# Loads in flight, the last store and the program's order in an RWKV-5 and SwiGLU kernel

## The chip, the cores and the metric

The kernel runs on one core of one Trainium2 chip. The metric is the device time of one execution in microseconds (us); lower is better. The core has a matrix engine (TensorE, PE in the profile; its weight loads are listed as PEld), VectorE (DVE), ScalarE (ACT), GpSimd (POOL) and SyncE (SP), which here issues nearly all transfers. Every engine works through its own queue of instructions in order. An instruction that must wait for another engine or for a transfer holds back everything behind it in its queue.

## The reference

An attention block without softmax (RWKV-5) is followed by a feed-forward block. There are 4 batches, 8 heads, 768 tokens and 48 channels a head, and all data are fp32 on the device.

```
for t in range(S):                                  # S = 768
    cur = einsum('bhd,bhe->bhde', u * k[t], v[t])
    y[t] = einsum('bhd,bhde->bhe', r[t], state + cur)
    state = w * state + einsum('bhd,bhe->bhde', k[t], v[t])

x = y as (3072 tokens, 384 features)
xn = x / sqrt(mean(x * x) + 1e-6) * rms_g
g, val = xn @ w_gate, xn @ w_val                    # 384 -> 1536
out = (g * sigmoid(g) * val) @ w_out                # 1536 -> 384
```

The weights w_gate, w_val and w_out reach the device as 64-bit floats, eight bytes each.

## The kernel before

The sequence is cut into 12 chunks of 64 tokens. With four batches a chunk holds 256 tokens. For each chunk `mixing(s)` does the attention. TensorE computes, with the names that the planner gives the steps:

- E: products of r with u*k, which give the diagonal of the scores (chunks 0 and 1 only; later chunks use VectorE steps called bonus1 to bonus3, which read the table `utab`)
- A: the scores inside the chunk. VectorE then writes the diagonal (d) and the masked scores (m) into the tile MT
- Y: the outputs, from V and MT and, after chunk 0, from the state ST carried over
- U: the update of the state, from V and KH, where KH is the tile TOK scaled by VectorE (step h)
- r, spread: sums of squares for the normalisation, and their distribution over the partitions

V, the tile for r and k by channel (`chan`, CH) and the tile for k by token (TOK) exist once each. A load for the next chunk can start only when the last reader of the chunk before has finished.

The feed-forward block then takes the 256 tokens of a chunk. Chunks 0 and 1 use plain products: the steps g (gate and value, `gate_val`, two TensorE steps each of 1.29 us) and P (`project`). The weights come in 26 pieces while these two chunks are computed. A piece (`piece`, line 395) is loaded by SP into one of six raw buffers. ACT computes a rounding part from the lower word (ulp), VectorE two steps from the upper word (bits1, bits2), and GpSimd adds the two (sum), so that an fp32 weight results. Pieces 0 to 17 are gate and value weights, pieces 18 to 25 the output weights (wot).

From chunk 2 on, two chunks are taken together. The first layer uses seven products instead of eight for each pair (steps f1 to f7 in `group`, six groups a pair), and the second layer likewise (P1 to P7 in `second_layer`). In this part the weights are read once more to check their range (`check`, steps "look"). The products use three banks of the accumulator memory, a, b and c, and a fourth tile, `at`, serves the attention.

The order of the program is written out by hand. Each step is registered with a planner (`Plan.add`, line 191): its engine, an estimated cost, the names it reads and writes, and a function that gives the instructions. The list `ORDER` (lines 83 to 155) then states in which order the 1532 steps are given to the engines. Since each engine works in order, the list decides what stands ahead of what in each queue, and at most how early a step can start. The planner's costs are used only to choose the number of warm-up products at the start. The waits between engines follow from which tiles are read and written.

A further wait is put on loads by hand. `InOrder.at_most` (line 164) lets a load go only when the load n places before it in the same sequence has landed:

```
made = give()
self.flying.append(made.ins)
if len(self.flying) > n:
    self.tc.add_manual_dep(made.ins, self.flying.pop(0).name, ...)
```

Loads of `chan`, TOK, V and the weight pieces pass through it, with n = IN_FLIGHT (line 258: `FIRST, IN_FLIGHT = 2, 2`). The load of `utab`, the moves of a few rows inside the on-chip memory (`move_heads`), the range checks and the stores do not, but they stand in the same SP queue.

At the end, `second_layer` of the last pair (chunks 10 and 11) works in two halves, js = 0 and js = 1. `result` (line 1171) stores each finished piece. For the last pair SP stores the first 64 rows and ACT the other 64; for other pairs SP stores both.

Of the kernel before, what the change touches and what calls it, by code (L numbers as in the profile page):

```python
# [72 lines left out]
def feature_order():  # L73
# [10 lines left out]
    0, 9, 1, 5, 14, 4, 2, 3, 6, 11, 12, 19, 39, 16, 8, 17, 40, 44, 41, 43, 24, 15, 49, 46, 47, 10, 42, 29, 20, 50, 74,  # L84
    45, 7, 51, 56, 13, 48, 53, 96, 57, 52, 18, 58, 54, 21, 55, 22, 63, 60, 26, 59, 27, 64, 23, 34, 25, 65, 81, 61, 66,
    62, 99, 28, 30, 67, 82, 119, 68, 109, 31, 69, 122, 70, 120, 75, 104, 36, 32, 86, 101, 76, 114, 83, 33, 84, 121,
    77, 100, 191, 35, 102, 78, 123, 80, 87, 98, 79, 71, 105, 190, 124, 37, 73, 127, 38, 187, 91, 130, 125, 103, 129,
    128, 92, 72, 126, 110, 106, 131, 107, 97, 115, 88, 108, 132, 151, 111, 133, 116, 152, 112, 117, 270, 153, 135,
    113, 380, 136, 206, 118, 137, 159, 154, 93, 134, 138, 160, 193, 196, 139, 155, 161, 192, 140, 145, 141, 142, 156,
    188, 215, 143, 148, 157, 162, 275, 144, 163, 214, 197, 164, 189, 194, 158, 171, 165, 211, 201, 146, 198, 172, 147,  # L90
    212, 199, 167, 173, 166, 195, 285, 174, 168, 202, 150, 213, 200, 89, 175, 149, 218, 176, 203, 169, 208, 221, 272,
    216, 237, 217, 183, 170, 268, 271, 204, 177, 184, 209, 178, 205, 280, 179, 185, 94, 186, 223, 273, 243, 267, 220,
    277, 90, 207, 244, 278, 222, 210, 180, 245, 224, 246, 219, 274, 251, 181, 281, 182, 252, 348, 349, 247, 253, 276,
    350, 279, 317, 225, 254, 287, 312, 226, 351, 248, 238, 229, 302, 263, 230, 361, 95, 255, 249, 282, 307, 227, 250,
    85, 256, 288, 228, 283, 264, 257, 258, 284, 265, 231, 239, 266, 259, 304, 286, 352, 260, 360, 309, 357, 305, 298,
    261, 232, 262, 290, 310, 289, 294, 233, 240, 303, 242, 269, 308, 299, 306, 241, 358, 295, 332, 311, 300, 301, 296,
    353, 318, 322, 297, 314, 291, 354, 319, 359, 337, 355, 387, 315, 292, 388, 327, 293, 374, 391, 389, 324, 408, 313,
    356, 323, 392, 320, 390, 407, 325, 362, 234, 316, 363, 399, 393, 321, 328, 236, 366, 364, 334, 367, 400, 326, 333,
    365, 339, 564, 561, 368, 342, 369, 329, 335, 340, 330, 562, 338, 343, 563, 331, 375, 370, 376, 336, 573, 341, 344,
    565, 371, 381, 382, 345, 406, 394, 346, 377, 568, 409, 379, 439, 378, 570, 395, 347, 587, 440, 384, 396, 410, 418,  # L100
    397, 566, 372, 383, 593, 401, 235, 373, 398, 567, 411, 413, 571, 594, 569, 402, 574, 412, 572, 385, 386, 575, 405,
    577, 441, 447, 442, 403, 414, 404, 444, 448, 576, 443, 445, 588, 449, 415, 579, 450, 446, 458, 620, 580, 453, 451,
    459, 454, 581, 460, 455, 452, 457, 466, 461, 621, 463, 467, 582, 468, 456, 462, 464, 477, 465, 583, 589, 472, 469,
    473, 474, 481, 470, 476, 478, 624, 479, 471, 485, 480, 622, 482, 486, 475, 416, 417, 487, 590, 483, 419, 421, 484,
    420, 496, 623, 630, 424, 488, 578, 491, 489, 595, 497, 498, 492, 591, 493, 490, 504, 495, 633, 499, 500, 505, 506,
    422, 494, 423, 501, 592, 632, 427, 515, 502, 425, 426, 503, 507, 430, 510, 508, 516, 517, 511, 646, 512, 509, 523,
    514, 518, 524, 625, 629, 525, 584, 520, 627, 513, 519, 428, 521, 429, 534, 522, 626, 433, 631, 431, 526, 628, 432,
    529, 527, 436, 535, 653, 536, 530, 531, 528, 533, 542, 537, 652, 543, 553, 634, 532, 554, 635, 539, 556, 636, 538,
    540, 544, 545, 647, 541, 637, 638, 548, 546, 639, 547, 549, 599, 551, 550, 437, 552, 596, 640, 555, 600, 641, 597,
    602, 559, 557, 434, 558, 435, 607, 598, 601, 648, 438, 797, 586, 642, 603, 643, 608, 798, 560, 611, 606, 604, 644,  # L110
    605, 585, 655, 645, 799, 656, 806, 610, 612, 807, 800, 803, 613, 649, 609, 654, 683, 801, 651, 685, 684, 614, 650,
    810, 691, 804, 615, 823, 809, 802, 692, 658, 830, 617, 805, 808, 829, 693, 657, 686, 618, 811, 856, 616, 857, 812,
    688, 813, 687, 689, 659, 694, 690, 619, 697, 695, 815, 696, 702, 816, 698, 703, 817, 699, 662, 704, 701, 710, 705,
    858, 707, 711, 700, 818, 706, 708, 712, 713, 709, 859, 660, 716, 661, 721, 717, 665, 714, 718, 826, 720, 715, 722,
    719, 723, 663, 664, 729, 724, 668, 860, 726, 730, 824, 731, 725, 727, 862, 825, 732, 728, 735, 733, 740, 736, 737,
    739, 742, 741, 863, 748, 743, 734, 882, 666, 745, 667, 738, 749, 671, 744, 746, 750, 751, 747, 759, 752, 827, 753,
    754, 760, 757, 761, 755, 828, 756, 669, 767, 758, 762, 869, 670, 861, 768, 674, 672, 764, 888, 673, 763, 765, 770,
    766, 769, 677, 773, 771, 831, 778, 774, 775, 777, 780, 779, 868, 782, 772, 781, 675, 776, 676, 783, 864, 866, 680,
    786, 784, 889, 865, 785, 789, 787, 788, 867, 792, 814, 793, 835, 790, 794, 678, 819, 791, 820, 836, 837, 870, 795,
    796, 832, 871, 839, 833, 679, 822, 874, 681, 682, 1033, 843, 872, 875, 1036, 821, 873, 842, 840, 841, 876, 844,  # L120
    846, 877, 834, 878, 879, 847, 891, 880, 881, 1037, 1046, 1045, 883, 838, 848, 849, 884, 892, 850, 894, 851, 885,
    1034, 852, 919, 1035, 921, 920, 887, 886, 1039, 927, 845, 1043, 1059, 895, 1038, 1040, 893, 1066, 928, 853, 922,
    929, 1041, 1065, 854, 938, 890, 924, 896, 855, 923, 925, 897, 930, 926, 933, 931, 939, 898, 940, 934, 901, 935,
    932, 937, 946, 941, 1042, 936, 942, 947, 948, 1044, 943, 957, 944, 945, 949, 952, 950, 959, 953, 1092, 954, 958,
    1047, 956, 951, 960, 955, 1060, 965, 1095, 1049, 962, 1048, 961, 963, 966, 968, 964, 899, 900, 1051, 971, 967,
    902, 969, 1061, 976, 1052, 972, 903, 973, 907, 1053, 977, 975, 978, 904, 970, 984, 979, 974, 981, 985, 1054, 980,
    982, 986, 987, 983, 1093, 990, 1094, 995, 988, 991, 989, 1062, 996, 1096, 992, 997, 908, 994, 1105, 1003, 905,
    998, 906, 1118, 1000, 1102, 910, 993, 1067, 1004, 999, 1001, 1101, 1005, 1006, 1002, 1125, 1099, 1064, 1098, 1014,
    1007, 1063, 909, 1009, 1015, 913, 1104, 1016, 1010, 1050, 1011, 1008, 1013, 1097, 1017, 911, 1124, 1103, 1022,
    1012, 1019, 1023, 912, 1018, 1020, 916, 1024, 1025, 1021, 914, 915, 1028, 1026, 1027, 1029, 1071, 1100, 1030,  # L130
    1055, 1031, 1072, 1056, 1073, 1106, 1032, 1068, 1119, 1075, 1058, 1069, 1107, 1120, 1110, 1111, 1108, 1079, 1269,
    1272, 917, 918, 1070, 1076, 1077, 1112, 1080, 1082, 1113, 1109, 1273, 1114, 1057, 1078, 1083, 1115, 1270, 1271,
    1074, 1127, 1279, 1084, 1117, 1085, 1282, 1086, 1116, 1087, 1121, 1275, 1081, 1128, 1155, 1130, 1156, 1088, 1089,
    1122, 1295, 1123, 1302, 1129, 1274, 1157, 1163, 1158, 1090, 1160, 1164, 1091, 1278, 1165, 1159, 1126, 1161, 1166,
    1162, 1134, 1174, 1167, 1280, 1131, 1169, 1175, 1168, 1176, 1170, 1171, 1173, 1182, 1177, 1178, 1183, 1281, 1184,
    1172, 1179, 1135, 1193, 1180, 1276, 1181, 1185, 1328, 1188, 1186, 1187, 1195, 1189, 1132, 1277, 1133, 1197, 1191,
    1190, 1137, 1194, 1192, 1301, 1196, 1283, 1329, 1285, 1198, 1201, 1199, 1200, 1204, 1202, 1330, 1136, 1203, 1207,
    1284, 1140, 1205, 1335, 1212, 1208, 1287, 1209, 1214, 1213, 1211, 1138, 1296, 1216, 1215, 1288, 1206, 1332, 1217,
    1139, 1210, 1289, 1218, 1220, 1141, 1219, 1331, 1223, 1221, 1142, 1222, 1226, 1146, 1224, 1143, 1231, 1227, 1286,
    1228, 1230, 1233, 1232, 1225, 1235, 1290, 1234, 1229, 1236, 1239, 1237, 1238, 1242, 1240, 1241, 1144, 1245, 1243,  # L140
# [104 lines left out]
def fast(ctx, tc, chan, tok, vpad, wka, wkb, wot, cols, u_row, out, bad):  # L245
# [9 lines left out]
    wide = wka.dtype == I64  # L255
    PIECE = NQ * CC * P

    FIRST, IN_FLIGHT = 2, 2
    NT = B * L
    const = ctx.enter_context(tc.tile_pool(name="const", bufs=1))  # L260
    work = ctx.enter_context(tc.tile_pool(name="work", bufs=2))
# [880 lines left out]
    def second_layer(s):  # L1142

        last = s + 2 == NS
# [636 lines left out]
```

## Time and profile before

| | |
|---|---|
| time, median of 3 runs | 608.51 us (605.94 to 609.43) |
| time of the profiled execution | 608.8 us |
| its span (first to last instruction) | 607.0 us |
| TensorE busy | 587.4 us |
| VectorE, ScalarE, GpSimd busy | 417.9, 297.1, 41.3 us |
| bytes moved, mean rate over the span | 62.99 MB, 104 GB/s |
| landing of a 576 KB weight piece, of V (512 KB), of chan (1024 KB), median | about 5.0, 4.3, 6.7 us |

All instructions of the kernel have line L178 in the profile, since `InOrder` gives them all from that line; they are told apart by the tiles that they write and read. A bracket after a timeline entry gives the idle time of the engine ahead of it and what released it. SPq and ACTq are the queues that issue transfers. "PEclk" is the share of full clock that TensorE was granted.

### The profile page before, as it was taken

The numbers are of one execution on the slowest core, as the hardware profiler recorded it, in microseconds if no ns is written. First come the engines' busy times: TensorE is split into PE (matmuls) and PEld (weight loads), VectorE is DVE, ScalarE is ACT, GpSimd is POOL, SyncE is SP. The second block draws the span as 40 slices with busy tenths as digits, with TensorE's granted clock in tenths as the row PEclk, the third lists the DMA queues.
The fourth block names the chain that finished last, engine by engine and source line by source line (L and its number), as shares of the span: only waits on it lengthen the run. The fifth ranks groups of instructions, "written<-read, shape, count | busy, mean of one in ns | idle before, by whom it ended". The sixth has DMA issues, their size and how long they took to land.

```text
span 607.0 us, 16431 instructions
## 1 busy us (share of the span) xinstructions
PE 587.4 (97%) x7202; PEld 516.4 (85%) x7202; DVE 417.9 (69%) x621; ACT 297.1 (49%) x721; POOL 41.3 (7%) x40
## 2 busy tenths in 40 slices
PE   5979999999999999999999999999999999999995
PEld 3768888667888899888899988899989899988895
DVE  6686886688777798566698466698567685455541
ACT  5653667635557554365465256564156762123200
POOL 3241322230000000000000000000000000000000
PEclk8689999999999999999999999999999999999999
DMA  6786754505132404411501602601422210200011
GB/s 209 243 257 218 252 172 143 179 2 208 53 94 72 163 2 119 143 54 50 218 22 36 240 1 60 235 15 34 154 96 87 65 44 23 70 27 28 1 28 31
DMA packets 22544, 62.99 MB, mean 104 GB/s; under 512 B 2976, under 2 KB 9792, under 8 KB 21056
## 3 DMA queue, kind: packets, MB, share of 16 engines
q1 hardware_dynamic: 21840, 61.46, 30.9%
q8 instruction: 58, 0.95, 0.7%
q10 hardware_dynamic: 624, 0.39, 0.2%
q14 instruction: 22, 0.18, 0.1%
HBM read 56.04 MB, written 4.72 MB: 100 GB/s over the span
## 4 chain that ended last, share of the span: by engine, by line
PE 92%; DMA 5%; ACT 1%; issue 0%; SPq 0%; DVE 0%; ACTq 0%
PE bank_b L178 32%; PE bank_a L178 26%; PE bank_c L178 24%; PE at L178 10%; DMA V<-in_vpad_dram 2%; DMA chan<-in_chan_dram 1%; DMA raw<-in_wot_dram 1%; DMA raw<-in_wkb_dram 1%; ACT ulp L178 0%; ACT ku L178 0%; ACT wk L178 0%; SPq L178 0%; ACT m L178 0%; DVE MT L178 0%; ACT h L178 0%
## 5 line engine op out<-in xcount | busy, mean ns | idle before, releaser
L178 DVE TENSOR_TENSOR gv<-bank_b,m 128x512 f32<-128x512 f32 x90 | 62.2, 691 | 66.5 <-PE bank_b L178 61.9
L178 ACT ACTIVATE gv<-gv 128x256 f32<-128x256 f32 (+1 forms) x60 | 30.7, 521 | 71.9 <-DVE gv L178 71.8
L178 DVE TENSOR_TENSOR gv<-bank_c,gv 128x512 f32<-128x512 f32 x60 | 41.5, 691 | 24.6 <-PE bank_c L178 24.1
L178 PE MATMUL bank_b<-xa,wa 64*128 64x256 f32 x444 | 56.2, 386 | 0.0
L178 PEld LDWEIGHTS bank_b<-xa,wa 64*128 64x128 f32 x444 | 43.3, 191 | 5.5 <-issue 0.2
L178 ACT COPY m<-bank_a 128x512 f32<-128x512 f32 (+1 forms) x35 | 19.9, 569 | 55.6 <-PE bank_a L178 33.5
L178 PE MATMUL bank_a<-wo,h 128*128 128x192 f32 x264 | 46.0, 330 | 0.5 <-ACT m L178 0.5
L178 PE MATMUL bank_a<-xa,wa 64*128 64x256 f32 x372 | 46.4, 379 | 0.0
L178 PE MATMUL bank_a<-xb,wb 64*128 64x256 f32 x372 | 45.7, 378 | 0.0
L178 PE MATMUL bank_b<-t,wb 64*128 64x256 f32 x360 | 44.3, 376 | 0.8 <-issue 0.8
L178 PE MATMUL bank_b<-t,s 64*128 64x256 f32 x360 | 44.8, 381 | 0.0
L178 PEld LDWEIGHTS bank_a<-wo,h 128*128 128x128 f32 x264 | 42.8, 190 | 2.3 <-issue 1.3
L178 PE MATMUL bank_c<-xb,s 64*128 64x256 f32 x360 | 44.3, 376 | 0.1
L178 PE MATMUL bank_c<-t,s 64*128 64x256 f32 x360 | 44.1, 377 | 0.0
L178 ACT ACTIVATE MT<-dmask,du 128x64 f32<-128x64 f32 x160 | 40.9, 336 | 5.3 <-DVE du L178 5.2
L178 ACT ACTIVATE rows_out<-rows_out 128x384 f32<-128x384 f32 x72 | 39.7, 557 | 2.3 <-DMA rows_out<-in_wot_dram 1.5
L178 PEld LDWEIGHTS bank_a<-xa,wa 64*128 64x128 f32 x372 | 36.1, 187 | 4.1 <-issue 0.2
L178 PEld LDWEIGHTS bank_a<-xb,wb 64*128 64x128 f32 x372 | 35.7, 187 | 4.5 <-issue 0.3
L178 PEld LDWEIGHTS bank_b<-t,wb 64*128 64x128 f32 x360 | 35.2, 187 | 4.8 <-issue 0.9
L178 DVE TENSOR_TENSOR h<-gv 128x256 f32<-128x256 f32 (+1 forms) x60 | 32.7, 552 | 9.2 <-ACT gv L178 9.2
L178 PEld LDWEIGHTS bank_c<-xb,s 64*128 64x128 f32 x360 | 35.4, 187 | 4.0 <-issue 0.3
L178 PEld LDWEIGHTS bank_b<-t,s 64*128 64x128 f32 x360 | 34.4, 187 | 5.0 <-issue 1.2
(179 smaller groups left out, 1079.1 us busy)
## 6 DMA issues: line engine op xcount, KB each, us to landing
chan<-in_chan_dram SPq DMA_DIRECT2D x11, 1024.0 KB, 6.7
TOK<-in_tok_dram SPq DMA_DIRECT2D x10, 768.0 KB, 5.2
V<-in_vpad_dram SPq DMA_DIRECT2D x12, 512.0 KB, 4.3
raw<-in_wot_dram SPq DMA_DIRECT2D x8, 576.0 KB, 5.1
rows_out<-in_wka_dram SPq DMA_DIRECT2D x12, 384.0 KB, 3.3
rows_out<-in_wkb_dram SPq DMA_DIRECT2D x12, 384.0 KB, 3.2
rows_out<-in_wot_dram SPq DMA_DIRECT2D x12, 384.0 KB, 3.1
out_dram<-rows_out SPq DMA_DIRECT2D x41, 96.0 KB, 2.2
```

Of the source, the lines that this page charges most:

```text
L178: return lambda *args, **kwargs: self.tc.keep_in_program_order(give(*args, **kwargs))
```

## The change

Three things change. The number of loads that may be in flight goes from two to four. Of the last pair, the last piece that is stored (k = 1, second half) is stored by ScalarE alone, both sets of 64 rows; all other stores stay where they were. And the list ORDER is another permutation: it has 1531 entries, since the last piece has one store step instead of two. The step names of the stores get individual keys, which only the planner reads.

```
-    FIRST, IN_FLIGHT = 2, 2
+    FIRST, IN_FLIGHT = 2, 4
...
-            if last:
-                add("SP", 0.6, keys, ["stored"], lambda: give((0,), sp), land=2.5, name="store")
-                add("ACT", 0.6, keys, ["stored'"], lambda: give((1,), act), land=2.5, name="store")
+            if last and k == 1 and js == (1,):
+                add("ACT", 1.0, keys, [f"stored {s} {k} {js}'"], lambda: give((0, 1), act), land=2.5, name="store")
+            elif last:
+                add("SP", 0.6, keys, [f"stored {s} {k} {js}"], lambda: give((0,), sp), land=2.5, name="store")
+                add("ACT", 0.6, keys, [f"stored {s} {k} {js}'"], lambda: give((1,), act), land=2.5, name="store")
             else:
-                add("SP", 1.2, keys, ["stored"], lambda: give((0, 1), sp), land=2.5, name="store")
+                add("SP", 1.2, keys, [f"stored {s} {k} {js}"], lambda: give((0, 1), sp), land=2.5, name="store")
```

What the new list does to each queue, by the names of the steps (the first ones, and the places that the prediction uses):

```
TensorE start   before  E0 A0 E0 Y0 A0 Y0 r0 r0 g g spread wk g E1 U0 g A1 g g Y1 ...
                after   E0 E0 A0 A0 Y0 Y0 r0 r0 g g spread wk g g U0 E1 A1 g g Y1 ...
TensorE, chunk 3   before  A3 g g g g g Y3 P(1,0) P(1,1) r3 P(0,0) ...
                   after   A3 P(0,0) Y3 P(1,0) P(1,1) r3 P(0,1) ...
TensorE end     before  P1 P1 flag P2 P6 P4 P7 P5 P6 P3 P7 P4 P5 P3
                after   flag P1 P1 P4 P6 P5 P7 P2 P6 P4 P7 P3 P5 P3
VectorE start   before  ... K R d m R d m bits1 2 ...
                after   ... K bits2 0 R R d m d m bits1 3 ...
VectorE, chunk 3   before  ... m3 bits2 20 hm h3 bits1 22 m3 ...
                   after   ... bits2 21 m3 m3 bits1 23 bits1 22 ...
SP loads        before  0, k0, 1, r0, 2, V0, 3, 4, TOK0, chan1, 5, 6, 8, 7, 9, 10, V1, utab, chan2, TOK1, 14, 13, move1, 11, TOK2 ...
                after   k0, 1, 0, r0, 2, V0, 3, 4, 6, chan1, 5, TOK0, 8, 7, 9, V1, TOK1, 11, 10, 12, TOK2, 14, move1, chan2, 15, 13, utab ...
```

Numbers alone are weight pieces; a number after k, r, V, TOK or chan is the chunk.

## The prediction

> **What bounds the kernel now.** I read the page first (busy times, slices, chain), then windows of 2 us for the first 64 us, then the timeline of the stretches that stood out, then the end. From the page:
>
> ```profile
> PE 587.4 (97%) x7202; PEld 516.4 (85%) x7202; DVE 417.9 (69%) x621; ACT 297.1 (49%) x721; POOL 41.3 (7%) x40
> ...
> PEclk8689999999999999999999999999999999999999
> ```
>
> TensorE is busy 587.4 of 607.0 us, so only 19.6 us are idle, and its work isn't changed. What an order or earlier loads can save is idle time and time at a lowered clock. The windows of 50 us show 48.92, 50.00, 49.25, 50.00 ... 49.93 us busy from 100 us on; nearly all the loss is in the first 46 us and at the end. The clock line says the same: 8, 6, 8 tenths in the first three slices, then 9. The 2 us windows (columns: window, length, busy us and instruction count of PE, PEld, DVE, ACT, POOL, then granted clock, DMA share, GB/s):
>
> ```profile
> 12.00:14.00 2.00, 0.67 (x27) 0.48 (x20) 1.95 (x5) 0.99 (x4) 0.74 (x1) 0.50 0.78 253
> 14.00:16.00 2.00, 1.88 (x70) 1.91 (x73) 0.00 (x0) 0.26 (x1) 0.00 (x0) 0.50 0.57 167
> ...
> 26.00:28.00 2.00, 1.54 (x10) 0.93 (x10) 0.93 (x3) 1.22 (x5) 0.93 (x1) 1.00 0.95 362
> ...
> 36.00:38.00 2.00, 1.41 (x14) 0.92 (x10) 1.97 (x5) 1.98 (x3) 0.72 (x2) 1.00 0.86 271
> 38.00:40.00 2.00, 0.00 (x0) 0.00 (x0) 2.00 (x3) 0.06 (x1) 0.78 (x1) 1.00 0.76 251
> 40.00:42.00 2.00, 1.35 (x93) 1.38 (x97) 2.00 (x3) 0.00 (x0) 1.73 (x1) 1.00 1.03 383
> 42.00:44.00 2.00, 2.00 (x55) 1.77 (x46) 1.56 (x3) 0.80 (x1) 1.42 (x2) 0.52 0.60 223
> 44.00:46.00 2.00, 2.00 (x14) 1.60 (x14) 0.00 (x0) 1.69 (x5) 0.00 (x0) 0.63 0.71 180
> ```
>
> The reader is to see two things. TensorE stands still from about 37.4 to 40.6, and afterwards runs at about half clock until 45. And the transfers mostly run at 170 to 270 GB/s, though single windows reach 362 and 383. The timeline names the waits:
>
> ```profile
> 14.12 1.56 PE L178 MATMUL at<-MT,V 64*64 64x64 f32 x48 [1.46 <-DMA V<-in_vpad_dram]
> 15.43 1.10 PE L178 MATMUL bank_a<-RR,chan 48*64 48x64 f32 x32
> ...
> 17.12 1.88 PE L178 MATMUL bank_c<-MT,V 64*64 64x64 f32 x48 [0.58 <-DVE MT L178]
> ...
> 40.65 1.16 PE L178 MATMUL at<-MT,V 64*64 64x64 f32 x64 [3.24 <-DMA V<-in_vpad_dram]
> ...
> 108.48 1.16 PE L178 MATMUL at<-MT,V 64*64 64x64 f32 x64 [1.08 <-ACT ulp L178]
> ```
>
> Both early waits are for V, the operand of the "Y" products of chunks 0 and 1. The third is Y of chunk 3, whose mask (ready at about 108.3) stood on VectorE behind a conversion that waited 3.10 us for a wot load. The SP timeline shows why V came late: V of chunk 0 was issued at 9.69, when the load before the last one had landed, and V of chunk 1 at 35.15, behind a weight load that was held the same way, although its buffer had been free since U of chunk 0 at 31.6.
>
> **What the Trainium skill says.** "DMA: Bandwidth & Descriptors", section "Anatomy of one DMA", gives a fixed part of about 2.0 us beside bytes over 436 GB/s. The trace agrees in kind: the 10 KB load of col took 1.7 us, the 576 KB loads 5.0. Two such loads in flight (1.18 MB in 4.9 us) give 241 GB/s, near the 261 GB/s measured from 20 to 40 us: the limit of two holds the rate down, not the memory. "TensorE: Matmul & The Clock Gate", part 1, says the clock falls to half after about 3.4 us idle and returns after about 3.4 us busy; here 3.2 us idle was followed by clocks of 0.52 and 0.63 for 4 us. "TensorEngine Tiling (Array Packing)", "Key Properties", says a change of tiling mode drains the engine; here the first product after an attention block takes 1.50 us instead of 1.29, so 0.2 us a change. "Runtime: NRT & Kernel Launch", "Instruction fetch mechanics", says a taken branch outside the fetched window forces a fetch; at the end here SP and ACT branch at 601.5 and go on at 605.1 and 605.3.
>
> **The change part by part.** The instruction lists of the two programs, engine by engine, hold the same work: 369 TensorE steps in both, and only the last stores are shared out differently.
>
> *Four loads in flight and the new order, first 46 us.* I walk the chain by hand. New issue order: k, wkb, wka, r of chunk 0 at once, then wka, V, wkb, wka. Up to r are 1.83 MB, up to V 2.75 MB. With the first load at 1.25, 1.7 us to the first landing and some 360 GB/s, r lands at about 8 to 9 (before 9.69), V at 10.6 to 12 (before 14.07). TensorE's order becomes E, E, A, A, Y, Y, so the second A no longer stands behind the Y that waits for V. VectorE then runs R, R, d, m, d, m without a hole: from 9.1, with the measured 1.21, 0.69, 0.74, 0.78, 0.74, 0.78, the last mask is ready at 14.0. Before, it came after A at 15.43 and Y started at 17.12. So the second Y starts at 14.0, 3.1 us earlier. It ends at 15.9 (1.88), its squares on ACT at 16.6, the second half of the row sums (half of 2.72) at 18.0; before, these ended at 21.64. The first weight product starts 3.6 us earlier and ends 3.5 earlier. Its exchanged copies (four of 0.51 after yT at 17.4) end at 19.5, before its second half needs them.
>
> From there to Y of chunk 1, TensorE had 11.3 us of work (26.1 to 37.4), so it is ready at about 33.9. V of chunk 1 can be issued once U of chunk 0 has read the old one, about 28.2, and a V load took 3.5 to 5.4 us: 31.7 to 33.6. The 3.24 us wait goes. TOK of chunk 0 is three places later on SP; 5.96 MB at 300 GB/s land at 23, and it is needed at 26. So Y starts 6.7 us earlier. Without the hole the clock stays up: Y took 2.51 in the chain and the pair after it 3.96, against 1.99 and 2.79 at full clock, 1.7 us in all. Together 8.4 us.
>
> Next late would be VectorE: it was busy 9.97 of 10 us from 30 to 40, and now has the same conversions to do some 8 us earlier, in one queue in which a conversion waiting for a load holds back masks and bank releases. Its total of 113 us in the first 150 leaves room (81% of 140), but not at every point. The bounds of this part are 0, if the time is lost again to such holds, and 8.4. I take three quarters, 6.3.
>
> *Y of chunk 3.* In the new VectorE list both masks stand ahead of the two waiting conversions, and one projection step is put before Y. The 1.08 us goes: 1.1 (bounds 0 and 1.1; next late would be the wot piece of that projection, whose loads were there by 91 before).
>
> *Mode changes.* Counted in both lists: 93 before, 89 after, at 0.2 us: 0.8. The chain of waits shows the price:
>
> ```profile
> 79.79 1.99 PE at L178 x128
> 81.78 1.50 PE bank_c L178 x12
> 83.28 1.29 PE bank_a L178 x12
> ```
>
> Elsewhere in the steady part TensorE has no hole to close, so its other moves count nothing; the banks' readers (VectorE 31 to 41 us busy per 50) hide them. If that cover were gone, each late bank costs one product, 1.3 us.
>
> *The last 35 us.* P1 is followed by P2 in the same bank, which waits for a copy on ACT:
>
> ```profile
> 576.32 0.48 ACT L178 COPY m<-bank_a 128x384 f32<-128x384 f32 x1 [2.19 <-PE bank_a L178]
> ...
> 576.85 4.17 PE L178 MATMUL bank_a<-wo,h 128*128 128x192 f32 x24 [0.51 <-ACT m L178]
> ```
>
> In the new order P4 comes between, and the flag product is moved ahead of P1. P4 reads what h23 wrote (before: by 575.2), P6 needs sum_2; the new VectorE order adds g2 before g1, so sum_2 ends at about 577.5 instead of 578.8, before P6 at 578.2. Gain 0.5 (bounds 0 and 0.6).
>
> *The last store.* Before, SP and ACT issued half each at 600.9, 0.47 and 0.50 us. Now ACT issues both, so its branch comes 0.5 us later, at 602.0; SP has branched earlier and does its waits meanwhile. Behind ACT's second issue stands only the end. Bounds: +0.5 (ACT's 3.8 us after the branch ends the program) and -0.5 (SP's eight semaphore steps of 605.1 to 605.6 were the last thing). I take +0.2. New names for the planner's store keys issue nothing.
>
> *Sum.* Against the profiled execution's own 608.8 us (span 607.0 and 1.8 around it): 608.8 - 6.3 - 1.1 - 0.8 - 0.5 + 0.2 = 600.3. The median of the runs, 608.51, is 0.3 from it; I leave 600.3. Had everything come in: 598.2.
>
> **The rivals.** *VectorE takes over.* Only the wait for V goes, 3.2 us and 0.3 of the clock; the conversions then set the pace and the head start melts. With 1.1 from mode changes and the end that is 4.6: 604.2. For it: 9.97 of 10. Against it: VectorE idles 5.47 us just after, until 49.1, waiting for TensorE.
>
> *Nothing moves.* The limit isn't what holds the loads; buffers are (six raw buffers, one V, one chan, one TOK). Then only mode changes and the end remain, 1.1: 607.7. For it: SP also waits for engines. Against it: in the first 20 us the SP timeline shows issues exactly at landings.
>
> *Slower.* The table of u (utab) is ten places later on SP, behind the load of chan for chunk 2, and VectorE's step bonus2, which reads it, now stands ahead of the release of the first bank of chunk 1's products. Up to utab are 14.2 MB. By the walk above TensorE is out of banks if that release comes after 56.2, so utab must land by 53.3 (bonus2 0.95, bonus3 0.94, state 0.54, release 0.42): 280 GB/s. Each us later is a us of TensorE, and such a hole costs 1.7 for the clock again. At 225 GB/s from 2.5 us on it lands at 65.6, 12.3 late: 598.2 + 14.0 = 612.2. The gain is eaten up below 238 GB/s, a little less than two loads in flight reached from 20 to 40 us.
>
> **How the numbers follow.** Forecast 600.3 (597 to 603): 0.60. VectorE takes over, 604.2 (603 to 606): 0.17. Nothing moves, 607.7: 0.15. Slower, 612.2: 0.08. A measurement of this kernel can tell about 0.5%, 3 us, from no change: faster is below 605.5, slower above 611.5. Faster: 0.60 + 0.14 + 0.01 = 0.75; same 0.03 + 0.14 = 0.17; slower 0.08. The range of 8 in 10 goes from 597 to 606.5: the first two cases and a little of the third.
>
> **What would show it.** Right: V of chunk 0 landed by 12, first weight product at 18, Y of chunk 1 by 34 to 36 without a wait for V, a clock of 1.00 from then on, f1 of chunk 2 (135.5 before) at 125 to 128, no ACT wait between P1 and what follows. Wrong: holes on TensorE between 40 and 110 released by VectorE, a DMA rate still near 240 GB/s, or conversions that wait for raw buffers.

## The result and the profile after

| | before | after |
|---|---|---|
| median of the runs made together | 608.94 us (605.94 to 609.43) | 599.2 us (596.28 to 599.99) |
| profiled execution | 608.8 us | 599.91 us |
| its span | 607.0 us | 598.2 us |
| mean granted clock | 0.985 | 0.993 |

The ratio of the times is 0.9842, with a 95% interval from 0.9802 to 0.9883. The forecast was 600.3 us. The profiled execution of the changed kernel was one of its longer ones, so its trace shows less than the medians do: 8.9 us of 9.7. The page of the changed kernel:

```profile
PE 583.4 (98%) x7202; PEld 512.6 (86%) x7202; DVE 411.2 (69%) x621; ACT 296.2 (50%) x721; POOL 46.2 (8%) x40
...
PEclk8989999999999999999999999999999999999999
```

TensorE is idle 14.8 us now (598.2 - 583.4), after 19.6. The second slice, which had a clock of 6 tenths, has 9, and the third has 8 as before. The 2 us windows, with the same columns as before, say where:

```profile
12.00:14.00 2.00, 1.89 (x94) 1.70 (x87) 2.00 (x7) 0.85 (x2) 1.71 (x2) 0.73 0.88 334
...
34.00:36.00 2.00, 1.10 (x77) 1.01 (x68) 1.97 (x4) 0.06 (x1) 0.00 (x0) 1.00 1.00 400
36.00:38.00 2.00, 1.17 (x41) 1.02 (x40) 1.60 (x3) 0.00 (x0) 1.32 (x1) 0.75 0.94 269
38.00:40.00 2.00, 2.00 (x13) 1.65 (x12) 0.00 (x0) 1.91 (x4) 1.62 (x2) 0.50 0.84 296
```

TensorE's timeline of the same stretch, where the two brackets with V are gone:

```profile
13.30 0.91 PE L178 MATMUL at<-MT,V 64*64 64x64 f32 x48
...
18.00 1.57 PE L178 MATMUL bank_a<-yT,wa 64*128 64x256 f32 x12
...
33.57 1.16 PE L178 MATMUL at<-MT,V 64*64 64x64 f32 x64
...
37.98 2.74 PE L178 MATMUL bank_b<-xa,wa 64*128 64x256 f32 x12
```

Y of chunk 1 starts at 33.57 instead of 40.65, at full clock. But from 36 to 40 the clock is 0.75 and 0.50, and the product that follows Y takes 2.74 us where it would take 1.57. The chain of waits (start, length, what) shows what lies between:

```profile
33.64 1.47 PE at L178 x89
35.10 1.73 issue
36.83 1.22 PE at L178 x39
38.05 3.96 PE bank_b L178 x23
```

(A shorter stop of this kind, 0.86 us, lies in the second Y of chunk 0, at 15.3.) In the middle of Y of chunk 1, after 89 of its 128 products, TensorE stands for 1.73 us. "issue" means that nothing which the profile shows is waited for. The kernel before has no such stop in this Y, and no step of the prediction has it.

The whole difference, from the start times of the same steps in both traces:

| stretch | before | after | gain |
|---|---|---|---|
| start to Y of chunk 1 | 40.65 | 33.57 | 7.1 |
| from there to the first g step of chunk 1 (g 1 0 0) | 15.56 | 17.54 | -2.0 |
| to Y of chunk 2 | 23.51 | 23.51 | 0 |
| to f1 of chunk 2 | 55.68 | 54.51 | 1.2 |
| to P1 of chunks 10 and 11 | 436.66 | 434.82 | 1.8 |
| to the last matmul | 28.13 | 27.24 | 0.9 |
| last matmul to the end of the span | 6.8 | 7.0 | -0.2 |

The sum is 8.8 us, the difference of the spans.

### The profile page after: what moved, and what is told of

The parts are those of the page before. It is cut to its first block, busy times and chain, and to the rows that moved or that the text cites. A ratio compares the mean times of both kernels' runs of the same rounds, so it can differ in the third digit from the quotient of the medians.

```text
span 598.2 us, 16446 instructions
## 1 busy us (share of the span) xinstructions
PE 583.4 (98%) x7202; PEld 512.6 (86%) x7202; DVE 411.2 (69%) x621; ACT 296.2 (50%) x721; POOL 46.2 (8%) x40
## 4 chain that ended last, share of the span: by engine, by line
PE 94%; DVE 2%; ACT 1%; issue 1%; DMA 1%; POOL 0%; SPq 0%; DVEq 0%; ACTq 0%
PE bank_b L178 32%; PE bank_a L178 26%; PE bank_c L178 26%; PE at L178 10%; DMA chan<-in_chan_dram 1%; DVE RR L178 1%; DVE bits L178 0%; ACT ku L178 0%; DVE MT L178 0%; ACT up L178 0%; DVE ms L178 0%; ACT ST L178 0%; DVE KH L178 0%; POOL ms L178 0%; SPq L178 0%
## 5 line engine op out<-in xcount | busy, mean ns | idle before, releaser
L178 ACT ACTIVATE gv<-gv 128x512 f32<-128x512 f32 (+1 forms) x60 | 31.2, 524 | 72.5 <-DVE gv L178 71.8
L178 PEld LDWEIGHTS bank_c<-t,s 64*128 64x128 f32 x360 | 34.6, 187 | 4.3 <-DVE h L178 0.3
```

The costliest lines, as they stand in the source:

```text
L178: return lambda *args, **kwargs: self.tc.keep_in_program_order(give(*args, **kwargs))
```

## The experiments

The whole set, with the intervals of the ratio to the kernel before. The column "f1" is the start of f1 of chunk 2 in the profiled execution, "steady" the time from there to P1 of the last pair, "end" from there to the last matmul.

| run | loads | order up to f1 | order after it | time | ratio, 95% | span | f1 | steady | end |
|---|---|---|---|---|---|---|---|---|---|
| before | 2 | old | old | 607.85 | | 607.0 | 135.4 | 436.7 | 28.1 |
| old_order_four | 4 | old | old | 600.76 | 0.9844 to 0.9937 | 595.0 | 124.3 | 435.5 | 28.1 |
| new_order_two | 2 | new | new | 606.9 | 0.9966 to 1.0007 | 602.4 | 134.1 | 434.8 | 27.2 |
| new_order_three | 3 | new | new | 600.94 | 0.9872 to 0.994 | 594.6 | 125.9 | 434.8 | 27.2 |
| front_new_rest_old | 4 | new | old | 600.93 | 0.9843 to 0.9926 | 599.3 | 127.5 | 436.9 | 28.1 |
| front_old_rest_new | 4 | old | new | 598.32 | 0.9819 to 0.9891 | 598.2 | 128.6 | 435.5 | 27.3 |
| new_order_old_store | 4 | new | new | 600.77 | 0.9849 to 0.9922 | 599.9 | 131.3 | 434.8 | 27.3 |
| hold_11 | 4 | new | new | 598.12 | 0.9821 to 0.9881 | 596.4 | 127.9 | 434.8 | 27.2 |

The runs were made on three chips, each beside the kernel before. Its median was 607.85 us for the first four, 606.83 for front_old_rest_new and new_order_old_store, and 606.48 for hold_11. So the times of different groups are compared by their ratios only. The spans and "f1" are those of one execution: it was the fastest of its kernel in old_order_four, new_order_two and new_order_three, and a longer one in the changed kernel.

The column "f1" differs by up to 4 us between executions of nearly the same program: f1 is at 129.1 in the changed kernel, at 131.3 with the old store alone and at 127.9 in hold_11. The clock of the first 20 us differs too: 0.91, 0.83 and 0.74 in these three. So the first columns of one profile don't tell two of these kernels apart; the intervals do, or the presence of a wait. The last two columns repeat to 0.1 us where no stop and no wait falls into them.

**The limit alone** (old_order_four).

```
-    FIRST, IN_FLIGHT = 2, 2
+    FIRST, IN_FLIGHT = 2, 4
```

> The order and the last store of before, four loads in flight. If the limit on loads is what gave the time (my theory for the front): V of chunk 0 lands by 12 us and V of chunk 1 by 36, Y of chunk 1 starts 4 to 6 us earlier than 40.65, and the whole is 4 to 6 us faster than before, 603 to 605. If the order gave it and the limit is only needed in company: the second A still stands behind Y, raw buffers hold the loads, and less than 2 us are gained, 607 to 609.

The time is 1.1% below the kernel before, 7.1 us where 4 to 6 were expected. The whole change gave 1.6%, and the two intervals overlap. The chain of waits of this run from 29 us on:

```profile
29.60 2.79 PE bank_c L178 x24
32.39 1.99 PE at L178 x128
34.38 2.79 PE bank_b L178 x24
```

Y of chunk 1 is ready at 32.3 with the old order too, there is no stop within its 128 products, and the clock stays up. The first weight product starts at 17.05, against 21.57. The wait ahead of Y of chunk 3 is gone as well: from Y of chunk 2 to f1 are 54.52 us.

**The order alone** (new_order_two): the changed kernel, its last store included, with the limit set back.

```
-    FIRST, IN_FLIGHT = 2, 4
+    FIRST, IN_FLIGHT = 2, 2
```

> Everything of the changed kernel but the limit, which is two. If the order alone gave the time: within 2 us of the changed kernel, 598 to 601. If the limit did: V of chunk 1 lands late again, TensorE waits 3 us or more ahead of Y of chunk 1, the table of u or a weight piece holds VectorE later on, and the time is 605 to 612.

The interval holds no change; the order alone is worth at most 0.34%, 2 us. The first weight product starts at 22.18, later than before (21.57). TensorE's timeline shows what came in place of the old wait for V:

```profile
36.08 1.16 PE L178 MATMUL at<-RR,chan 48*64 48x64 f32 x64 [2.12 <-DVE chan L178]
37.17 2.90 PE L178 MATMUL bank_c<-yT,wa 64*128 64x256 f32 x12
...
41.65 1.16 PE L178 MATMUL at<-MT,V 64*64 64x64 f32 x64
```

A of chunk 1 waits for VectorE's work on chan, the clock falls, and the product behind it takes 2.90 us. Y of chunk 1 starts a microsecond later than in the kernel before. From Y of chunk 2 to f1 are 54.51 us, so the order alone removes the wait ahead of Y of chunk 3, just as the limit alone does.

**Three loads** (new_order_three): the same line with `IN_FLIGHT = 3`.

> The changed kernel with three loads in flight. In the changed kernel TensorE stood 1.73 us inside Y of chunk 1 with no wait that the profile shows, at the first instruction of a block of 256 of its own queue (number 1217). If loads in flight slow the fetch of instructions, this hole shrinks with three, below 1 us, and the clock stays up; the time is the same or up to 2 us better, 597 to 599. If the depth of the queue of loads has nothing to do with the hole, it stays at 1.5 us or more wherever Y of chunk 1 still starts before 34.5 us, and the time is 599 to 602.

Three give what four give, within what the timing tells. The stop in Y is gone, as the theory had it, but the 597 to 599 us expected with it did not come. A of chunk 1 waits 2.39 us here, so the front isn't a clean comparison with four.

**The two halves of the order** (front_new_rest_old, front_old_rest_new). Both have four loads in flight. The first takes the new list up to the first f2 of chunk 2 and the old list and store from there; the second the reverse.

```
 ORDER = [
-    <new list, 1531 entries>
+    <new list up to the first f2 of chunk 2> <old list from there>
```

> Four loads in flight; the new order up to the first step f2 of chunk 2, the old order and the old last store from there. If the gain sits in the front: f1 of chunk 2 starts at about 129 as in the changed kernel (135.4 before) and the time is 601 to 603. If the steady part and the end gave a good part of it (I read 1.8 us and 0.9 us from the traces), the time is about 2.5 us above the changed kernel's, 601.7; a rival that puts everything in the front gives 599 to 600.

> Four loads in flight; the old order up to the first f2 of chunk 2, the new order and the new store from there. Theory (the limit gives the front, the new rest closes the small holes of the steady part): the front as with the old order and four in flight (Y of chunk 1 at about 32.3, g 0 1 0 at about 34.3, f1 of chunk 2 at about 124), f1 to the last P1 in about 434.8 as in the changed kernel instead of 436.7, no ACT wait behind P1; span 592 to 595, ratio to the kernel before 0.975 to 0.986. Rival (the new front order is itself worth something with four loads): f1 of chunk 2 not before 129, span 598 or more.

The times can't be told from each other or from the changed kernel's. In the second the front of the profiled execution was slow from the start (clock 0.80 in the first 20 us, against 0.91 in the run named warm_16 below), so f1 came at 128.6 instead of the 124 expected, and the span was 598.2 us, where the theory had 592 to 595 and the rival 598 or more. This pair doesn't decide between them. The columns "steady" and "end" are its use: the end is 28.1 us with the old list and 27.2 to 27.3 with the new one in every run, so the 0.9 us belongs to the order of the last part. The steady part varies for another reason: the long value of front_new_rest_old has a stop of 1.08 us at 240.8, and the 435.5 of front_old_rest_new a wait for VectorE at 147.0, just behind the seam of its two lists, which costs 0.7. The kernel before has such stops too, as its chain shows:

```profile
248.61 0.21 PE bank_b L178
248.82 0.75 issue
249.57 1.35 PE bank_b L178 x10
```

**The stop moves with the count of instructions** (warm_32, warm_16). These stops stand at related places in TensorE's own list of instructions (weight loads, products and semaphore steps counted from the start): the larger ones are at numbers 449 and 1217 in the changed kernel, 6593 and 11713 in the kernel before, 1217 and 6593 in front_new_rest_old. Each leaves the remainder 193 when divided by 256. The page of the profile lists the transfers by which instructions are fetched as "q8 instruction: 58" packets and 0.95 MB, 16 KB each; 58 times 256 is 14,848, and TensorE has 14,452 instructions. "Runtime: NRT & Kernel Launch" of the Trainium skill, section "Instruction fetch mechanics", says that instructions are fetched in blocks of 16 KiB, 256 of them, and that this is mostly hidden. The trace agrees with the size of the blocks. If the stops are waits for such a fetch, it isn't hidden there. To test it, the eight warm-up products were split, so that all later instructions of TensorE stand 112 or 48 numbers later. In the run warm_32:

```
-                pe.matmul(bank_of["b"][:, 0], ones, free_dims(ones, (0, 4), (1, P)), start=True, stop=True)
+                for j in range(8):
+                    pe.matmul(bank_of["b"][:, 0, j * 64 : (j + 1) * 64], ones, ones[:, 0:64], start=True, stop=True)
```

> The changed kernel, with each of the eight warm-up products split into eight of 64 columns: the same work, but TensorE's instructions stand 112 numbers later in its queue. In the changed kernel TensorE stands still for 1.7 us ahead of its instruction number 1217, 89 products into Y of chunk 1. Theory (the stop is a wait for the next 256 instructions): any stop stands at number 1217 again, now about 33 products into Y, or it is gone because the fetch falls among slower products. Rival (the stop belongs to the product or its operands): it stays 89 products into Y, at number 1329.

> As the run before with the warm-up products split into four of 128 columns each: 48 numbers later. Theory (the stop is a wait for the next 256 instructions): the stop stands at number 1217, now about 65 products into Y of chunk 1. Rival (it belongs to the product): 89 products into Y, at number 1265.

Chain of waits of warm_32, and below it of warm_16:

```profile
37.80 0.66 PE at L178 x33
38.46 0.84 issue
39.30 1.59 PE at L178 x93
```

```profile
33.16 1.13 PE at L178 x65
34.29 1.69 issue
35.98 1.11 PE at L178 x63
```

The stop comes after 33 products of Y, and after 65, where the theory put it: at number 1217 both times. So it isn't tied to the product or its operands. Each of the two ran once (601.01 and 602.49 us), so their times aren't compared. (In warm_32 the 64 small warm-up products took 13.92 us and made everything start 5 us later. The profile has no record of the clock before 21.1 us there; a group of 32 E products took 1.08 us, as at half clock in the changed kernel, against 0.68 in warm_16. After that the clock stayed at 1.00, and f1 came only 1.7 us later.) In warm_16 a stop of 2.52 us fell into the steady part as well, at 387.8, number 10433, remainder 193, and the half clock after it, from 391.1 to 394.5, makes its steady part longer still.

**Why the fetch is late** (hold_11). In the traces the fetch packets come one to a block: one between numbers 705 and 961, the next between 961 and 1217. The time from number 961 to its packet, the rate of all transfers in between, and the largest time between two starts at number 1217:

| run | number 961 | packet | later by | GB/s in between | stop |
|---|---|---|---|---|---|
| new_order_three | 30.78 | 31.36 | 0.6 | 21 | none |
| new_order_two | 36.80 | 38.32 | 1.5 | 249 | none |
| old_order_four | 29.15 | 30.91 | 1.8 | 291 | none |
| front_old_rest_new | 33.46 | 35.40 | 1.9 | 234 | none |
| before | 34.16 | 37.13 | 3.0 | 251 | none (TensorE waits for V meanwhile) |
| warm_16 | 29.56 | 33.30 | 3.7 | 276 | 1.9 |
| after | 30.39 | 34.30 | 3.9 | 340 | 1.9 |
| new_order_old_store | 32.45 | 36.51 | 4.1 | 303 | 2.0 |
| warm_32 | 32.91 | 37.00 | 4.1 | 278 | 1.1 |
| front_new_rest_old | 29.32 | 34.54 | 5.2 | 316 | 3.0 |

Late packets go with the new order and four loads. In all these five runs V, TOK and weight pieces 11, 10 and 12 are issued before the packet comes. In the changed kernel four of these loads are issued before number 961 and the last at 32.66:

```profile
27.68 0.33 SPq L178 DMA_DIRECT2D V<-in_vpad_dram  x1
28.10 0.39 SPq L178 DMA_DIRECT2D TOK<-in_tok_dram  x1
29.30 0.33 SPq L178 DMA_DIRECT2D raw<-in_wkb_dram  x1
29.68 3.31 SPq L178 DMA_DIRECT2D raw<-in_wka_dram  x2
```

In old_order_four the small table of u and chan stand in the place of those pieces. The rate alone doesn't part the two groups (291 GB/s there, 276 in warm_16). The experiment holds piece 11, and so 10 and 12 behind it, until V has landed:

```
+        if behind:
+            self.tc.add_manual_dep(made.ins, self.flying[-1 - behind].name, ...)
...
-sp.at_most(IN_FLIGHT, lambda: sp.dma_start(out=raw, in_=part))
+sp.at_most(IN_FLIGHT, lambda: sp.dma_start(out=raw, in_=part), behind=2 if n == 11 else 0)
```

> The changed kernel with one wait added: weight piece 11 (and with it 10 and 12, which stand behind it on SP) goes only when V of chunk 1 has landed. So fewer bytes are under way when TensorE passes its instruction number 961 and the next 256 instructions are fetched. In the runs with the new order and four loads in flight the fetch packet came 3.7 to 5.2 us after that point and TensorE stood 1.0 to 3.0 us at number 1217; with the old order and four loads it came after 1.8 to 1.9 us and TensorE did not stand. Theory (the fetch waits behind the loads): the packet comes within 2.5 us, no stop over 0.3 us at number 1217, Y of chunk 1 takes 2.0 to 2.3 us instead of 4.4. Rival (the fetch is late for another reason, such as where it stands in TensorE's queue): the packet again after 3.5 us or more and a stop of 1 us or more. The time: 0 to 4 us below the changed kernel's by the theory, if the pieces that come some 2 us later are waited for by nothing on TensorE's path; which the timing can only just tell.

Its SP timeline and its chain of waits:

```profile
29.94 0.33 SPq L183 DMA_DIRECT2D V<-in_vpad_dram  x1
30.36 1.36 SPq L183 DMA_DIRECT2D TOK<-in_tok_dram  x1
33.77 0.33 SPq L183 DMA_DIRECT2D raw<-in_wkb_dram  x1
```

```profile
33.22 2.79 PE bank_c L183 x24
36.01 1.99 PE at L183 x128
37.99 2.79 PE bank_b L183 x24
```

Number 961 passes at 32.76 and the packet comes at 34.62, 1.9 us later, with 212 GB/s in between. The stop in Y is gone, Y takes 1.99 us in one piece, and the products behind it run at full clock. (The stop at number 449, which lies ahead of the added wait, is still there.) From Y of chunk 1 to g 1 0 0 are 13.94 us, against 17.54: 3.6 us of this stretch came back. But Y itself started at 35.94, 2.4 us later than in the changed kernel. V was already issued 2.3 us later, and TensorE had half clock from 9.6 to 23.3 us here, from 9.7 to 13.1 in the changed kernel. The fair partner is therefore new_order_old_store, whose front was late as well: V issued at 29.68, number 961 at 32.45, pieces not held, and the packet 4.1 us later with a stop of 2.0. This is one profile on each side, and what the fetch waits for among the loads isn't shown. The ratio, 0.9851, is the same as that of the changed kernel within the interval.

**The last store** (new_order_old_store): the changed kernel with the last piece shared by SP and ACT again.

```
-            if last and k == 1 and js == (1,):
-                add("ACT", 1.0, keys, [f"stored {s} {k} {js}'"], lambda: give((0, 1), act), land=2.5, name="store")
-            elif last:
+            if last:
```

> The changed kernel with the last store shared by SP and ACT as before. Theory (the store costs 0.2): from the last VectorE instruction to the end of the span 6.1 instead of 6.26 us; the time is the changed kernel's within 0.5 us, which the timing can't tell. Rival (ACT's store alone shortens or lengthens the end): more than 0.5 us in that stretch, either sign.

From the end of VectorE's last instruction to the end of the span are 5.8 us here, and 6.0 to 6.3 in the three other runs with the old store (before, front_new_rest_old, old_order_four). With the new store the seven runs give 5.6 to 6.3 (the changed kernel 6.3, new_order_two 5.6). Neither the 0.2 of the theory nor the rival's half microsecond can be told from the spread; the timing shows nothing either.

## Why the prediction was right, and where not

*The total.* 8.9 us between the profiled executions, 8.5 forecast. The parts fit less well than the sum: the front gave 1.2 us less than forecast, the steady part 1.0 and the end 0.4 more. That these cancel was luck.

*The front.* The landmarks came as walked: no wait for V, the first weight product at 18.00 (18.0), Y of chunk 1 at 33.57 (34 to 36, 7.1 us earlier where 6.7 was worked out). But the clock did not stay at 1.00, and f1 of chunk 2 came at 129.13 instead of 125 to 128. Of 8.4 walked, 6.3 were taken, and the front gave 5.1 up to g 1 0 0. The step that failed is the reason given for taking three quarters: a hold of conversions on VectorE. From g 1 0 0 to Y of chunk 2 both kernels take 23.51 us, so VectorE held nothing. Y began 0.4 us earlier than walked, and behind it 3.6 us were lost: the stop of 1.73 us, 0.7 for the rest of Y, and 1.2 for the pair of products behind it, which lasted 3.96 us at half clock instead of 2.79. hold_11, which takes the stop away, needs 13.94 us for the stretch from Y to g 1 0 0, where the kernel before took 15.56: that is 1.6 us less, and the 1.7 forecast for the clock was right where nothing interrupts. So the reduction was made for the wrong reason, and was still 1.2 too small (6.3 taken, 5.1 measured). The prediction's rule for the clock, a fall after about 3.4 us idle, did not warn of this: here the clock fell after a stop of 1.73.

*Which part earns it.* The prediction walked the limit and the order together and gave the order a share: the second A "no longer stands behind the Y that waits for V". The order alone moves the first weight product 0.6 us later, the limit alone 4.5 us earlier. Once V lands in time, nothing stands behind Y's wait in either order.

*Y of chunk 3.* Forecast 1.1, measured 1.2. It was put down to VectorE's new list; either part removes it alone.

*Mode changes.* 0.8 was forecast. The steady part gained 1.8, but mostly from something else. Around its stops at 248.8 and 455.0, which the prediction passed over, the kernel before loses 1.6 us against its usual pace of 1.29 us for 12 products; old_order_four loses 0.4 around one stop. Without these both are at 435.1, so 0.3 us remain for the order. In the traces TensorE's work from f1 to the last P1 falls into 63 stretches of one mode before and 62 after: one change fewer, 0.2 us. The other changes that were counted lie in the front and at the end. All three traces with the old list after f1 have a stop there, at number 6593 or 11713. None of the six with the new list there has one, leaving the two runs with split warm-up products aside. So the order may have moved these fetches to better places, which wasn't tested.

*The last 35 us.* Forecast 0.5, measured 0.9 in every run with the new list. The copy on ACT still waits for P1, but TensorE is in its next product by then:

```profile
563.95 4.17 PE L178 MATMUL bank_a<-wo,h 128*128 128x192 f32 x24
...
568.15 0.48 ACT L178 COPY m<-bank_a 128x384 f32<-128x384 f32 x1 [3.06 <-PE bank_a L178]
```

The size was worked out from the ACT wait of 0.51 alone; the flag product's move ahead of P1 was listed without a price. Counted from the product ahead of P1 (570.66 and 562.43) the gain is 0.8, since the flag product stood behind P1 only before. What of the rest is the flag's wasn't tried.

*The last store.* Forecast +0.2. The changed kernel's own trace has it (6.3 against 6.1 us), but over all runs no difference is left.

*The rivals.* "Nothing moves" falls with old_order_four. "Slower" through the table of u did not come: TensorE waits for nothing between 40 and 130 us in the changed kernel, and the windows from 44 to 48 us move 356 and 408 GB/s. "VectorE takes over" has its place in new_order_two and new_order_three, where A of chunk 1 waits 2.12 and 2.39 us for VectorE, but not in the changed kernel.

*Left open.* Whether loads also make the fetches late in the steady part. The transfers are mostly idle there, but not at the stops: the packet came 3.1 us after number 6337 in the kernel before, with 265 GB/s in between, and 2.8 us after number 10177 in warm_16, with 293. No load was held there. Also open is why the clock fell to half after the stop in the changed kernel but not after a stop of 1.69 us in warm_16. In all the traces the recorded clock changes only at multiples of 3.41 us from its first record. In the step ahead of the fall TensorE was busy 1.68 us; in the step of warm_16 that holds the stop it was 1.72. Other steps don't give a clean limit: the clock fell after 2.6 and 3.0 us busy in two of them, and stayed up after 1.5 in another.

## What to carry to other kernels

When a change mixes a limit on loads with a new order, run each alone: here a limit of four loads with the old order gave 1.1% of the 1.6%, and the order alone nothing that could be measured. The rest is less than the timing can tell. Once the visible waits of a stretch of small products are gone, look for idle time marked "issue" at equal remainders of the engine's instruction count; here it was a wait for a fetch of instructions, late where large loads were issued shortly before. Holding back loads that nobody waits for yet removed it in the one trace in which it was tried, though not measurably from the time.

## What the runs showed of the hardware

Instruction fetch was not always hidden. Every stop of this kind in the eleven traces, 21 with 0.28 to 3.0 us between two starts, ended 1.3 to 1.6 us after the end of a fetch packet; in the changed kernel the packet ended at 35.25 and TensorE went on at 36.83. Instructions 961 to 1217, which hold the first part of Y, take 4.4 to 4.5 us where nothing stops. A packet lasts about 0.95 us (0.9 to 1.3). From these numbers the packet may come about 2 us late at most, an estimate: at 1.9 us (hold_11, front_old_rest_new) there was no stop, at 3.7 to 5.2 us there were stops of 1.1 to 3.0. A block that is done sooner stops even with the transfers nearly idle: in hold_11 the packet came 0.6 us after number 705 with 25 GB/s in between, and number 961 came 3.3 us after number 705, after a stop of 0.5. Where a block takes long, a late packet costs nothing: 2.5 us after number 9153 in the changed kernel, where the block lasts 9.0 us.
